# Attention and FFN on one core: each engine's order made with the timeline model

## The chip, the cores and the metric

The program runs on one core of a Trainium2 chip. A core has five engines that work side by side, each through its own list of instructions, strictly in order: TensorE (PE, matrix products), VectorE (DVE), ScalarE (ACT), GpSimd (POOL) and SyncE (SP, which here only issues transfers). They wait for one another by semaphores. The metric is the time of one execution on the device in microseconds (us), as the median of several runs.

## The reference

The input is a batch of 8, with 8 heads, 576 tokens and 64 numbers per head. Every head gets two softmax attentions, one among neighbours (a band of |distance| < 4) and one over the sequence pooled by 4. Their sum, as a matrix of 4608 tokens by 512, goes through a feed-forward network with a piecewise quadratic activation.

```python
q_d, k_d, v_d = mean over groups of 4 tokens of q, k, v
out_up = np.repeat(sm_attn(q_d, k_d, v_d), 4, axis=2)
mask = np.abs(pos[:, None] - pos[None, :]) < 4
scores = np.where(mask, scale * q @ k.T, -1e9)
x = (out_up + softmax(scores) @ v).reshape(4608, 512)
h = x @ w_in                                   # 512 -> 2048
g = np.where(h >= 1, h, np.where(h <= -1, 0, (h + 1) ** 2 / 4))
return g @ w_out                               # 2048 -> 512
```

Everything is float32 except the FFN's weights: they are float64 in the host's memory and the kernel converts them from their two words.

## The kernel before, in words

**Pairs.** Attention works on 32 pairs of two heads: pair n is pair n % 4 of batch n // 4. `attention` is a generator; each `yield` ends a stage, and the stages of a pair run over all engines:

- DVE pools q and k to `qd` and `kd` (L161, L165). PE writes the local scores `sl_ps` (L186) and the pooled scores `sp_ps` (L200). Then SP issues the next pair's q and k loads (L133; `q_sb` and `k_sb` have one buffer each).
- The local softmax: DVE adds the band (L221) and takes the maximum `mxl` (L224), POOL subtracts it (L225), ACT takes the exponential (L226). The pooled one: DVE L236, L237, L238, ACT L240. DVE sums and divides (L249, L250, L253, L254, L258).
- PE transposes the local part, `tl` (L272), which ACT copies to `al` (L276); and the pooled part, `tp` (L284), which ACT copies to `ap` (L290).
- PE multiplies with the values: `pl` (L306) and `pp` (L318). ACT scales `pp` to `xd` (L327), DVE adds to `x` (L329), ACT casts it to `xh` (L336), POOL takes the rest `xl` (L337). `xh` and `xl` are a ring of two batches and the FFN's input, in two parts of less precision.

After the first pairs, `sl_ps`, `tl_ps`, `tp_ps` and `pl_ps` share one PSUM tile (tag a2, one buffer), so that each waits until the one before has been read.

**FFN.** 12 chunks of 384 tokens by 16 slices of the hidden layer make 192 steps, numbered here 0 to 191; h48 is the first product of step 48. A step's first product is 12 matmuls into `h_ps` (L447, two buffers): for each of the four pairs of the batch `xh` twice and `xl` once. ACT takes relu and square (L458, L459), DVE bounds it (L460), which frees `h_ps`; ACT casts to `gh` (L463), POOL takes the rest `gl` (L464). The second product is 9 matmuls into three banks `o_ps` (L478): six from `gh`, three from `gl`. At a chunk's end ACT copies `o_ps` to `osb` (L483), and SP stores it (L484).

A chunk needs all pairs of its tokens' batch. A new batch is needed first at step 16 (pairs 4 to 7), 48 (8 to 11), 64 (12 to 15), 96, 112, 144 and 160 (28 to 31).

**Weights.** SP loads 32 raw slices (L348); ACT (L360, L362, L368), DVE (L365, L366) and POOL (L369) convert them, two for each of the steps 0 to 15.

**What sets the order.** The program emits its work in a hand-written order: `BEFORE_STEPS` and `FIRST_STEPS` for the start, then a loop that emits, for each step, some stages of a pair (`attn_step`), h of a step and the second product of an earlier one. Code under `high_priority` (the activation in `mm1`) is ranked ahead. The library's scheduler then makes the list of each engine from that: it takes the emitted order as a priority and runs a model of the machine to tell which instruction is ready when.

## Time and profile before

| | us |
|---|---|
| median of 2 runs | 1011.65 |
| lowest, highest | 1011.37, 1011.93 |
| span of the profiled execution | 1009.0 |
| mean of PE's clock in it | 0.985 of full |

The span runs from the first to the last instruction; the times of the runs are some 2.65 us longer than it. In the profile a matmul is listed with its tiles, written ahead of `<-`, and its shape; two passes of the array are counted for a matmul of attention, so that the 20 matmuls of L186 appear as 40. Busy time is not the same as need: an engine that works beside PE costs nothing as long as PE does not wait for it. That is why the prediction asks, of each place, what PE stands waiting for.

### The profile page before, as it was taken

To read this page: it belongs to the slowest core of one execution; us is meant where nothing else is said; L and a number is where in the kernel's file an instruction comes from. 1 tells how busy PE (TensorE), PEld (TensorE's weight loads), DVE (VectorE), ACT (ScalarE), POOL (GpSimd) and SP (SyncE) were. 2 spreads that over 40 slices of the span, in tenths; PEclk is the share of its full clock that TensorE was granted. 3 is DMA by queue.
4 is the path that set the end of the run, shared out by engine and by line. 5 is a ranking of instruction groups with operands and counts; after the bars stand their busy time and mean duration, and the time that the engine had idled before them with its cause. 6 is when DMAs were issued, how large, how long until landed. Compare 5 with 4: busy or idle time off the path is not lost.

```text
span 1009.0 us, 18511 instructions
## 1 busy us (share of the span) xinstructions
PE 967.4 (96%) x7612; PEld 845.8 (84%) x7612; DVE 386.9 (38%) x668; ACT 488.3 (48%) x1063; POOL 391.1 (39%) x359
## 2 busy tenths in 40 slices
PE   4688899999999999999999999999999999999997
PEld 4467678998888888998888888999888888899996
DVE  5879872114443443113444434112434444111111
ACT  5678754334545445334445544434544454433433
POOL 3668674224333443222434334222334433222221
PEclk9799899999999999999999999999999999999999
DMA  8685121003112221001221212101212220000000
GB/s 291 212 296 196 50 64 41 1 1 104 50 49 81 74 67 63 1 1 55 73 69 61 75 49 68 39 1 31 74 49 66 91 71 14 32 1 1 32 1 32
DMA packets 26533, 66.24 MB, mean 66 GB/s; under 512 B 3152, under 2 KB 3152, under 8 KB 26448
## 3 DMA queue, kind: packets, MB, share of 16 engines
q1 hardware_dynamic: 26448, 65.06, 19.8%
q8 instruction: 60, 0.98, 0.4%
q14 instruction: 25, 0.20, 0.1%
HBM read 55.61 MB, written 9.44 MB: 64 GB/s over the span
## 4 chain that ended last, share of the span: by engine, by line
PE 79%; DVE 6%; issue 6%; POOL 3%; ACT 3%; DMA 2%; SPq 0%; POOLq 0%; DVEq 0%; ACTq 0%
PE h_ps L447 35%; PE o_ps L478 33%; PE tp_ps L284 2%; PE sl_ps L186 2%; PE pl_ps L306 2%; PE tl_ps L272 2%; DVE m L366 2%; PE pp_ps L318 2%; POOL gl L464 2%; DVE m L365 1%; PE sp_ps L200 1%; DMA first_o<-kT 1%; DMA raw_i<-w_in 1%; POOL sl L225 1%; ACT sp L240 0%
## 5 line engine op out<-in xcount | busy, mean ns | idle before, releaser
L447 PE MATMUL h_ps<-xh,w_i 128*128 128x384 f32 x1536 | 405.7, 344 | 0.0
L464 POOL TENSOR_TENSOR gl<-u,gh 128x384 fp32r<-128x384 f32 x192 | 195.8, 1020 | 525.9 <-ACT gh L463 385.6
L478 PE MATMUL o_ps<-w_o,gh 128*128 128x512 f32 x1152 | 358.2, 392 | 0.4 <-ACT gh L463 0.4
L447 PEld LDWEIGHTS h_ps<-xh,w_i 128*128 128x128 f32 x1536 | 277.0, 188 | 20.8 <-issue 10.9
L460 DVE SCALAR_TENSOR_TENSOR u<-h_ps,u 128x384 f32<-128x384 f32 x192 | 106.8, 556 | 453.4 <-ACT u L459 425.4
L447 PE MATMUL h_ps<-xl,w_i 128*128 128x384 f32 x768 | 262.4, 342 | 0.0
L478 PEld LDWEIGHTS o_ps<-w_o,gh 128*128 128x128 f32 x1152 | 214.2, 188 | 32.6 <-ACT gh L463 1.2
L478 PE MATMUL o_ps<-w_o,gl 128*128 128x512 f32 x576 | 226.2, 393 | 4.3 <-POOL gl L464 4.3
L458 ACT ACTIVATE u<-h_ps 128x384 f32<-128x384 f32 x192 | 94.4, 492 | 271.9 <-PE h_ps L447 271.8
L463 ACT CAST gh<-u 128x384 fp32r<-128x384 f32 x192 | 98.6, 513 | 114.8 <-DVE u L460 114.8
L447 PEld LDWEIGHTS h_ps<-xl,w_i 128*128 128x128 f32 x768 | 144.6, 188 | 0.7 <-POOL xl L337 0.3
L478 PEld LDWEIGHTS o_ps<-w_o,gl 128*128 128x128 f32 x576 | 108.4, 188 | 30.0 <-POOL gl L464 7.1
L459 ACT ACTIVATE u<-u 128x384 f32<-128x384 f32 x192 | 100.3, 523 | 5.0
L225 POOL TENSOR_TENSOR sl<-sl,mxl 128x640 f32<-128x640 f32 x28 | 35.5, 1267 | 43.8 <-DVE mxl L224 43.8
L337 POOL TENSOR_TENSOR xl<-x,xh 128x576 fp32r<-128x576 f32 x32 | 46.4, 1451 | 8.4 <-ACT xh L336 8.4
L329 DVE TENSOR_TENSOR x<-pl_ps,xd 128x576 f32<-128x576 f32 x32 | 24.2, 756 | 59.6 <-ACT xd L327 59.6
L264 POOL TENSOR_TENSOR vh<-vp_sb 72x512 f32<-72x512 f32 x32 | 41.3, 1291 | 10.4 <-DMA vp_sb<-vp 8.3
L221 DVE TENSOR_TENSOR sl<-sl_ps,band_sb 128x640 f32<-128x640 f32 x28 | 23.1, 824 | 41.6 <-PE sl_ps L200 41.6
L249 DVE TENSOR_REDUCE sp_ps<-sl 128x10 f32<-128x640 f32 x32 | 26.4, 825 | 30.1 <-ACT sp L240 30.1
L306 PEld LDWEIGHTS pl_ps<-al,v_sb 64*64 64x64 f32 x1280 | 23.9, 144 | 15.7 <-issue 8.8
L284 PE MATMUL tp_ps<-ident,sp 128*72 128x128 f32 x192 | 29.5, 293 | 4.5 <-ACT sp L240 2.5
L272 PE MATMUL tl_ps<-ident,sl 128*128 128x128 f32 x160 | 25.1, 291 | 8.9 <-POOL sl L254 5.3
(67 smaller groups left out, 777.2 us busy)
## 6 DMA issues: line engine op xcount, KB each, us to landing
v_sb<-vw SPq DMA_DIRECT2D x32, 320.0 KB
vp_sb<-vp SPq DMA_DIRECT2D x32, 288.0 KB
out<-osb SPq DMA_DIRECT2D x36, 256.0 KB
raw_i<-w_in SPq DMA_DIRECT2D x16, 512.0 KB
raw_o<-w_out SPq DMA_DIRECT2D x16, 512.0 KB
q_sb<-qT SPq DMA_DIRECT2D x28, 288.0 KB
k_sb<-kT SPq DMA_DIRECT2D x28, 288.0 KB
first_i<-qT SPq DMA_DIRECT2D x4, 288.0 KB
```

Of the source, the lines that this page charges most:

```text
L225: nc.gpsimd.tensor_tensor(slf, slf, ml_n, op=ALU.subtract)
L272: nc.tensor.transpose(tl_v[:, g * P : (g + 1) * P], sl[:, g].rearrange("p r c -> p (r c)"), ident)
L284: nc.tensor.transpose(tp_v[:, kb, i, :], sp[:, i, kb * KB : (kb + 1) * KB], ident if i < 2 else swapped,)
L306: nc.tensor.matmul(pl_v[hs, o : o + OUT_LEN[i]], v[rs, 2 * g + h, :], al[rs, g, c0 : c0 + OUT_LEN[i]], start=True, stop=True,)
L337: nc.gpsimd.tensor_tensor(xl[:, p, r0 : r0 + S], x, xh[:, p, r0 : r0 + S], op=ALU.subtract)
L447: nc.tensor.matmul(h[:, :TCH], wi[:, wt, cc * P : (cc + 1) * P], xt[:, cc, ts], start=(n == 0), stop=(n == 3 * NCC - 1),)
L458: nc.scalar.activation(u, h[:, :TCH], AF.Relu, bias=0.5, scale=0.5)
L459: nc.scalar.activation(u, u, AF.Square)
L460: nc.vector.scalar_tensor_tensor(u, h[:, :TCH], 1.0, u, op0=ALU.max, op1=ALU.min)
L463: nc.scalar.copy(gh, u)
L464: nc.gpsimd.tensor_tensor(gl, u, gh, op=ALU.subtract)
L478: nc.tensor.matmul(o, gt[:, ts], wo[:, wt, :], start=f == 0 and n == 0, stop=f == NFC - 1 and n == 2)
```

## The change

The scheduler ran with its default model; now it runs with the library's timeline model of the machine. No line of the kernel's work is touched.

```diff
-    with tile.TileContext(nc) as tc:
+    with tile.TileContext(nc, schedule_with_timeline_sim=True) as tc:
         attention_then_ffn(tc, *args, out)
```

Each engine has the same instructions as before, and only their order differs. Three places show how. The names are those of the tiles, with the numbers of their buffers where rows would read alike; x20 counts equal instructions in a row.

PE, before, the end of pair 11, the last that step 48 needs (`h_ps_3145` and `h_ps_3209` are the first products of steps 46 and 47):

```order
L272 MATMUL tl_ps_3128<-ident_73,sl_3043 128x128 x5
L447 MATMUL h_ps_3145<-xh_86,w_i14_1634 128x384 x2
L447 MATMUL h_ps_3145<-xl_87,w_i14_1634 128x384
L447 MATMUL h_ps_3145<-xh_86,w_i14_1634 128x384 x2
L284 MATMUL tp_ps_3136<-ident_73,sp_3049 72x128 x6
L447 MATMUL h_ps_3145<-xl_87,w_i14_1634 128x384
...
L478 MATMUL o_ps2_2425<-w_o13_1585,gl_3116 128x512
L306 MATMUL pl_ps_3175<-al_3134,v_sb_2965 64x61
...
L318 MATMUL pp_ps_3198<-ap_3143,vd_3064 64x144 x4
L447 MATMUL h_ps_3209<-xh_86,w_i15_1697 128x384 x2
```

PE, now, the same pair (`h_ps_3299` is the first product of step 48; its first nine matmuls and those of step 49 stand earlier):

```order
L478 MATMUL o_ps2_2425<-w_o15_1705,gl_3227 128x512
L272 MATMUL tl_ps_3128<-ident_73,sl_3043 128x128 x5
L284 MATMUL tp_ps_3136<-ident_73,sp_3049 72x128 x6
L306 MATMUL pl_ps_3175<-al_3134,v_sb_2965 64x61
...
L318 MATMUL pp_ps_3198<-ap_3143,vd_3064 64x144 x4
L186 MATMUL sl_ps_3242<-k_sb_3041,q_sb_3039 64x64 x20
L200 MATMUL sp_ps_3263<-kd_3240,qd_84 64x144 x2
...
L447 MATMUL h_ps_3299<-xh_86,w_i0_225 128x384 x2
L447 MATMUL h_ps_3299<-xl_87,w_i0_225 128x384
```

The tail of pair 11 and the scores of pair 12 have moved from steps 46 and 48 to one piece between the second product of step 47 and the rest of steps 48 and 49, with no matmul of the FFN in it. Steps 96 (pair 19) and 144 (pair 27) look the same.

DVE, before, from the end of pair 11 on (`u_3222` belongs to step 47, `u_3312` to step 48; `qd` here is that of pair 13):

```order
L329 TENSOR_TENSOR x_3205<-pl_ps_3175,xd_3203 128x576
L165 TENSOR_REDUCE kd_3240<-k_sb_3041 128x144
L460 SCALAR_TENSOR_TENSOR u_3222<-h_ps_3209,u_3222 128x384
L221 TENSOR_TENSOR sl_3274<-sl_ps_3242,band_sb_78 128x640
L236 TENSOR_REDUCE sp_ps_3263<-sl_ps_3242 128x1
L224 TENSOR_REDUCE mxl_3275<-sl_3274 128x10
L237 TENSOR_REDUCE sp_ps_3263<-sp_ps_3263 128x2
L161 TENSOR_REDUCE qd_84<-q_sb_3270 128x144
L238 TENSOR_SCALAR mxp_3281<-sp_ps_3263 128x3
L460 SCALAR_TENSOR_TENSOR u_3312<-h_ps_3299,u_3312 128x384
```

DVE, now:

```order
L329 TENSOR_TENSOR x_3205<-pl_ps_3175,xd_3203 128x576
L165 TENSOR_REDUCE kd_3240<-k_sb_3041 128x144
L221 TENSOR_TENSOR sl_3274<-sl_ps_3242,band_sb_78 128x640
L236 TENSOR_REDUCE sp_ps_3263<-sl_ps_3242 128x1
L161 TENSOR_REDUCE qd_84<-q_sb_3270 128x144
L224 TENSOR_REDUCE mxl_3275<-sl_3274 128x10
L237 TENSOR_REDUCE sp_ps_3263<-sp_ps_3263 128x2
L238 TENSOR_SCALAR mxp_3281<-sp_ps_3263 128x3
L460 SCALAR_TENSOR_TENSOR u_3312<-h_ps_3299,u_3312 128x384
```

`qd` has moved two instructions ahead of the maximum and stands, as before, ahead of L460 of step 48, which PE's step 50 waits for; the score products that release its load are now later on PE. On ACT the relu of a chunk's first step is followed by the three `osb` copies and then by its square.

PE, before, the end of pair 15, the last that step 64 needs (`h_ps_4081` is step 62, `h_ps_4145` step 63, `h_ps_4175` step 64; pair 16 follows at step 79):

```order
L272 MATMUL tl_ps_4064<-ident_73,sl_3979 128x128 x5
L447 MATMUL h_ps_4081<-xh_86,w_i14_1634 128x384 x2
...
L284 MATMUL tp_ps_4072<-ident_73,sp_3985 72x128 x6
...
L318 MATMUL pp_ps_4134<-ap_4079,vd_4000 64x144 x4
L447 MATMUL h_ps_4145<-xh_86,w_i15_1697 128x384 x2
...
L447 MATMUL h_ps_4175<-xh_86,w_i0_225 128x384 x2
```

PE, now, from the end of pair 14 (`pp_ps_3903`) over all of pair 15 to the scores of pair 16 (`sl_ps_4670`); `h_ps_4214` is step 65 and `h_ps_4247` step 66:

```order
L318 MATMUL pp_ps_3903<-ap_3848,vd_3769 64x144 x4
L186 MATMUL sl_ps_3947<-k_sb_3746,q_sb_3744 64x64 x20
...
L447 MATMUL h_ps_4175<-xh_86,w_i0_225 128x384 x2
L447 MATMUL h_ps_4214<-xh_86,w_i1_308 128x384 x2
...
L272 MATMUL tl_ps_4064<-ident_73,sl_3979 128x128 x5
L284 MATMUL tp_ps_4072<-ident_73,sp_3985 72x128 x6
...
L318 MATMUL pp_ps_4134<-ap_4079,vd_4000 64x144 x4
L186 MATMUL sl_ps_4670<-k_sb_3977,q_sb_3975 64x64 x16
...
L447 MATMUL h_ps_4247<-xh_86,w_i2_431 128x384 x2
```

Pair 15, which ended two steps ahead of its need, now begins with its scores when steps 64 and 65 already stand half done, and the only FFN matmuls from there to step 66 are the remaining twelve of steps 64 and 65. Step 112 (pairs 22 and 23) and step 160 (30 and 31) look the same, the latter without a next pair; step 16 has pairs 6 and 7 so.

Two more moves, in words. On SP, at the start, the v load of pair 1 stood 22nd with six of the weight loads ahead of it, and now stands 41st with 25 ahead; the loads of v for pairs 2 and 3 come after it. In the steady steps PE now runs h two steps ahead of the second product, and takes the six `gh` matmuls of it ahead of the three `gl` ones at many steps, where before each bank's three stood together; attention breaks the FFN's matmuls into 136 pieces where there were 117. At the end of the program the second products of steps 189, 190 and 191 all follow h191.

## The prediction

> **What bounds the kernel now.** I read the page first: the busy line, the granted clock by slices, and the chain of work that ended last.
>
> ```profile
> span 1009.0 us, 18511 instructions
> PE 967.4 (96%) x7612; PEld 845.8 (84%) x7612; DVE 386.9 (38%) x668; ACT 488.3 (48%) x1063; POOL 391.1 (39%) x359
> PEclk9799899999999999999999999999999999999999
> PE 79%; DVE 6%; issue 6%; POOL 3%; ACT 3%; DMA 2%; SPq 0%; POOLq 0%; DVEq 0%; ACTq 0%
> ```
>
> TensorE is busy for 967.4 of 1009.0 us and carries 79% of the chain. Then busy time by stage (columns: window, its length, busy time of PE, PEld, DVE, ACT, POOL with counts, PE's clock, DMA share, GB/s).
>
> ```profile
> 0.00:150.00 150.00, 115.65 (x1203) 92.91 (x1204) 118.75 (x176) 103.44 (x224) 96.02 (x82) 0.90 0.55 186
> 25.00:50.00 25.00, 15.67 (x240) 11.40 (x240) 21.27 (x34) 17.01 (x39) 17.03 (x14) 0.70 0.64 209
> 100.00:150.00 50.00, 43.44 (x410) 36.05 (x411) 41.48 (x56) 33.06 (x72) 33.92 (x28) 0.93 0.19 56
> 150.00:952.00 802.00, 799.88 (x6155) 706.65 (x6155) 261.47 (x481) 364.81 (x800) 282.28 (x265) 1.00 0.15 47
> ```
>
> From 150 to 952 us PE misses only 2.1 us: nothing can be won there, and every wait that a new order opens on PE is paid in full. Only the start has air: PE idles 34.4 us of the first 150.
>
> Last the timeline of one ordinary pair of heads in that stretch (start, duration, engine, line, tiles, count). It gives the latency of each link of the attention chain.
>
> ```profile
> 268.94 0.86 PE L186 MATMUL sl_ps<-k_sb,q_sb 64*64 64x64 f32 x38
> 270.28 0.62 PE L447 MATMUL h_ps<-xh,w_i 128*128 128x384 f32 x2
> 274.55 0.52 PE L447 MATMUL h_ps<-xh,w_i 128*128 128x384 f32 x2
> 276.67 0.62 PE L478 MATMUL o_ps<-w_o,gh 128*128 128x512 f32 x2
> 278.71 0.71 PE L272 MATMUL tl_ps<-ident,sl 128*128 128x128 f32 x5
> 279.17 0.60 PE L447 MATMUL h_ps<-xh,w_i 128*128 128x384 f32 x2
> 280.20 0.85 PE L284 MATMUL tp_ps<-ident,sp 128*72 128x128 f32 x6
> 280.81 0.42 PE L447 MATMUL h_ps<-xl,w_i 128*128 128x384 f32 x1
> 284.29 0.80 PE L306 MATMUL pl_ps<-al,v_sb 64*64 64x61 f32 x40
> 285.02 0.71 PE L318 MATMUL pp_ps<-ap,vd 72*64 72x144 f32 x8
> ...
> 270.18 0.82 DVE L221 TENSOR_TENSOR sl<-sl_ps,band_sb 128x640 f32<-128x640 f32 x1 [1.50 <-PE sl_ps L200]
> 271.14 0.81 DVE L224 TENSOR_REDUCE mxl<-sl 128x10 f32<-128x640 f32 x1
> 271.87 0.46 DVE L237 TENSOR_REDUCE sp_ps<-sp_ps 128x2 f32<-128x288 f32 x1
> 273.39 0.75 DVE L161 TENSOR_REDUCE qd<-q_sb 128x144 f32<-128x576 f32 x1 [1.07 <-DMA q_sb<-qT]
> 276.06 0.83 DVE L249 TENSOR_REDUCE sp_ps<-sl 128x10 f32<-128x640 f32 x1 [0.93 <-ACT sp L240]
> 277.42 0.82 DVE L254 TENSOR_TENSOR sl<-sl,sp_ps 128x640 f32<-128x640 f32 x1
> 283.48 0.56 DVE L460 SCALAR_TENSOR_TENSOR u<-h_ps,u 128x384 f32<-128x384 f32 x1 [4.26 <-ACT u L459]
> 286.17 0.76 DVE L329 TENSOR_TENSOR x<-pl_ps,xd 128x576 f32<-128x576 f32 x1 [2.13 <-ACT xd L327]
> ...
> 273.32 0.74 ACT L226 ACTIVATE sl<-sl 128x640 f32<-128x640 f32 x1
> 279.45 0.70 ACT L276 COPY al<-tl_ps 128x640 f32<-128x640 f32 x1 [0.20 <-PE tl_ps L272]
> 281.09 0.64 ACT L290 COPY ap<-tp_ps 72x576 f32<-72x576 f32 x1 [0.94 <-PE tp_ps L284]
> 282.33 0.49 ACT L458 ACTIVATE u<-h_ps 128x384 f32<-128x384 f32 x1 [0.61 <-PE h_ps L447]
> 285.78 0.29 ACT L327 ACTIVATE xd<-pp_ps 128x144 f32<-128x144 f32 x1 [1.19 <-PE pp_ps L318]
> 286.96 0.68 ACT L336 CAST xh<-x 128x576 fp32r<-128x576 f32 x1 [0.89 <-DVE x L329]
> ...
> 272.03 1.26 POOL L225 TENSOR_TENSOR sl<-sl,mxl 128x640 f32<-128x640 f32 x1 [1.68 <-DVE mxl L224]
> 287.74 1.45 POOL L337 TENSOR_TENSOR xl<-x,xh 128x576 fp32r<-128x576 f32 x1
> ...
> 269.90 0.34 SPq L133 DMA_DIRECT2D q_sb<-qT  x1
> ```
>
> Read it as links. tl to tp 1.49 us (280.20 − 278.71, al between). tp to the end of ap 1.53. pl with pp 1.44. From the end of pp (285.73): x is done 1.20 later, xh 1.91, xl 3.46. sl_ps fills in 0.86, the score group holds PE 1.34. The next q load is issued as L186 ends (269.80) and lands 3.59 later, when qd starts. Here all of this lies behind FFN matmuls, which cost 2.12 per 12 (274.55 to 276.67, 0.177 each).
>
> **The change, part by part.** No instruction is added or dropped; only orders change. So I go through PE's new order and ask at each break: how much PE work stands between an instruction and what it needs, and how long does the chain above take? The difference is a wait.
>
> *Light places, steps 48, 96, 144.* tl, tp, pl, pp of the batch's last pair and sl of the next stand together. Start tl at 0: tp 1.49, pl 3.02, pp ends 4.46, x done 5.66, and only then may sl start (one PSUM tile serves both); its L186 part ends 6.52. xl is done at 7.92, so h48 and h49 end near 8.7. But h50 needs the buffer that DVE's L460 for step 48 frees, and DVE now has qd of the next pair ahead of that, behind a load issued at 6.5 that lands at 10.11. Then qd 0.75, L224 0.73, L237 0.46, L460 0.56, with L238 between: h50 starts at 12.7. PE's own work there is tl 0.46, tp 0.61, pl and pp 1.44, sl 1.34, six h 1.06, together 4.9. Wait 7.8, three times: **23.4**. ACT's relu of step 48 ends near 9.2, and the three osb copies now queued ahead of its square take at most al's 0.70 each: square done by 11.9, just before DVE asks for it, so nothing more.
>
> *Heavy places, steps 64 and 112.* Here the last two pairs stand so. From the end of pp[14]: sl[15] at 1.20, L186 ends 2.06, q lands 5.65, qd to 6.40, L224 to 7.21, POOL's subtract 1.26, exp 0.74. From exp's start to L249 it was 2.74 above, with a square and a cast of the FFN between; I take 1.7 without. L249 to the end of L254 is 2.18: tl[15] at 12.4. Then 4.46 to the end of pp, 1.20 to x, sl[16] with four h inside to about 19.6, load 3.59, DVE 2.5: h66 at 25.5. PE work is 7.3. Wait 18.2, twice: **36.4**.
>
> *Step 160.* No q load follows pair 31: sl[31] at 1.20, L221 at 2.44, L224 done 4.21, subtract and exp as before, tl[31] at 9.5, pp ends 13.9, xl 17.4, and relu to L460 1.71 more (282.33 to 284.04): h162 at 19.3. PE work 6.0. Wait **13.3**.
>
> *Step 16.* Pairs 6 and 7 are left to the end likewise. From sl[7] to tl[7] 8.3 us, with 2.8 of PE work; the tail of pair 7 as a light place: 12.2 of waits. Before, the same pairs already left PE idle 6.6 of the 50 us from 100 to 150, which is given back: **5.6**.
>
> *Start.* SP's queue now has 19 more weight loads ahead of pair 1's v.
>
> ```profile
> 27.86 0.33 SPq L139 DMA_DIRECT2D v_sb<-vw  x1
> 60.81 1.00 SPq L348 DMA_DIRECT2D raw_o<-w_out  x1
> 61.86 0.99 SPq L348 DMA_DIRECT2D raw_i<-w_in  x1
> ```
>
> A weight load follows the last by 1.05 us, so that v is issued some 20 us later, near 48; pl of pairs 1 to 3 share one v buffer and follow at a load's 3.6 us each, to about 60. Against that the conversions stand earlier on ACT and fill time. I take **+5**, between −10 and +16.
>
> *Breaks.* PE's FFN runs are broken by attention 136 times where it was 117. The five h from 279.17 to 280.20 took 1.03 instead of 0.885: 0.15 each, **+2.8**. The rest of the FFN order (two h ahead, the six gh before the three gl) keeps each gh and gl behind more PE work than its chain takes: nothing, and if that cover were short by the 0.5 of a cast it would be 0.5 a step. The end, where the last three second matmuls run without an h between: nothing, at most 1 either way.
>
> *Clock.* This row shows what a wait costs beyond itself:
>
> ```profile
> 122.06 1.40 PE L284 MATMUL tp_ps<-ident,sp 128*72 128x128 f32 x6 [1.90 <-ACT al L276]
> 124.54 1.01 PE L447 MATMUL h_ps<-xh,w_i 128*128 128x384 f32 x2
> ```
>
> After 1.90 us idle the same tp takes 1.40 against 0.85 and two h take 1.01 against 0.52: half speed, about 1.9 us lost before it recovers (0.55 on the tp, 0.49 on the two h, the rest on the eight sp between them). In the window 25:50, with PE at 63%, the granted clock was 0.70. The places hold some 11 waits over 1.9 us (one in each light place, two or three in each other): **+21**, between 10 and 27. [...]
>
> *Sum.* 23.4 + 36.4 + 13.3 + 5.6 + 5 + 2.8 + 21 = 107.5. On the span of 1009.0 that is 1116.5. The runs' median, 1011.65, is 2.65 above the span, so 1119, rounded **1120 us**.
>
> **Rivals.**
> - *The places cost less* (1060 to 1095). Engines that wait may answer quicker than in the loaded stretch, and a q load alone may land sooner: 1.5 us at seven loads, a third of the clock term, a start that comes out even.
> - *The start or the clock costs more* (1140 to 1180). The start's upper end (11 more) and the clock's (6 more) give 1137. If all PE work inside the places, some 50 us (three times 4.9, twice 7.3, 6.0 and about 14 at step 16), ran at half speed and lay on the chain, it would be 50 in place of 21: 1149, with the start 1160. For it: 0.70 in 25:50. Against: the slow stretch after 122.06 is short.
> - *Hardly a change* (992 to 1032). The waits would have to be under 20 in sum, four fifths of the chains gone. The links are data, each measured with its waiter idle; only L224 to L249 and the load have slack. Nor is the order the same: the light places have no matmul between tl and tp where before there were five.
> - *Faster* (about 985). The start's idle PE is the only thing to win: 34.4 us, of which early weights and conversions might fill 26. It decides only if the eight places together cost less than what it saves; one light place alone is 7.8 and the two heavy ones 36.
>
> **How the numbers follow.** Forecast 0.60 (1095 to 1145), less 0.20, more 0.10, hardly a change 0.06, faster by over 2% 0.04. 2% is about what a measurement of this kernel can tell from no change. Slower 0.90, same 0.06, faster 0.04. The range of eight in ten leaves out the last two, half of "more" and a little of "less": low 1070 (no clock term beyond 10, start −10, quicker loads), high 1150.
>
> **What would show it.** After: PE idle in front of tl, tp, pl, sl and h at steps 16, 48, 64, 96, 112, 144 and 160, about 8 us at the light ones and 18 at 64 and 112, with DVE's qd waiting for a q load inside; full busy between; PEclk below 9 in those slices; the first h some 5 us later. Wrong if those places show PE busy through, if the idle time lies in the steady steps instead, or if DVE's qd does not wait.

## The result, and the profile after

| | before | after |
|---|---|---|
| median of 2 runs, us | 1011.65 | 1148.25 |
| lowest, highest | 1011.37, 1011.93 | 1147.9, 1148.6 |
| span of the profiled execution | 1009.0 | 1146.8 |
| mean of PE's clock in it | 0.985 | 0.926 |

The kernel became slower: 1.1354 times the time before, with an interval of 1.1326 to 1.1381. The forecast was 1120 with a range of 1070 to 1150, so the time lies in the range, close to its upper end, and 28 us above the forecast. It is where the prediction's second rival ("the start or the clock costs more", 1140 to 1180) was to be.

The page of the changed kernel, the same lines as before: span, busy time, PE's clock in 40 slices, shares of the chain of waits.

```profile
span 1146.8 us, 18502 instructions
PE 1022.5 (89%) x7612; PEld 880.9 (77%) x7612; DVE 381.2 (33%) x668; ACT 482.0 (42%) x1063; POOL 392.3 (34%) x359
...
PEclk7679895999998998899999899699999899879999
...
PE 81%; DMA 7%; DVE 6%; ACT 3%; issue 1%; POOL 1%; SPq 0%; ACTq 0%; DVEq 0%; POOLq 0%
```

In the chain of waits transfers have gone from 2% to 7%. PE's idle time was 41.6 us before (1009.0 less 967.4) and is 124.3 now (1146.8 less 1022.5): 82.7 more. And the same 7612 matmul records keep PE busy 55.1 us longer (1022.5 less 967.4). Together these are the 137.8 by which the span grew. The busy time by stage shows where they are (columns as in the prediction's first such table; the fourth row, 342 to 370, is step 48).

```profile
0.00:158.00 158.00, 117.14 (x1055) 97.28 (x1056) 109.44 (x165) 100.13 (x215) 92.41 (x79) 0.81 0.48 165
158.00:204.00 46.00, 32.15 (x308) 25.76 (x307) 16.73 (x31) 16.26 (x39) 16.35 (x15) 0.74 0.25 77
204.00:342.00 138.00, 138.00 (x938) 119.39 (x937) 33.74 (x62) 54.37 (x117) 42.16 (x40) 1.00 0.11 33
342.00:370.00 28.00, 20.90 (x181) 17.92 (x180) 11.61 (x22) 11.79 (x30) 8.73 (x8) 0.88 0.23 72
...
429.00:478.00 49.00, 32.89 (x309) 26.44 (x309) 16.27 (x30) 15.54 (x38) 14.40 (x13) 0.79 0.22 67
...
975.00:1016.00 41.00, 28.58 (x242) 22.95 (x242) 9.39 (x17) 13.79 (x31) 10.26 (x10) 0.75 0.08 28
```

The rows stand for step 16 (158 to 204), a light place (342 to 370), a heavy one (429 to 478) and step 160 (975 to 1016). PE idles 13.85, 7.10, 16.11 and 12.42 us in them, and its clock is below full there. In between, as from 204 to 342, it does not idle at all. Ahead of 158 us it idles 40.86. So the air is in the start and at the places that the prediction named, and nowhere in the steady steps.

Step 48, all engines, cut to the rows that carry the chain (start, duration, engine, line, tiles; in brackets the idle time before and what ended it; the transposes `tl` and `tp` are listed once for each instruction, the other matmuls of attention twice):

```profile
348.05 0.71 PE L272 MATMUL tl_ps<-ident,sl 128*128 128x128 f32 x5
349.54 0.85 PE L284 MATMUL tp_ps<-ident,sp 128*72 128x128 f32 x6 [0.78 <-ACT al L276]
351.11 0.80 PE L306 MATMUL pl_ps<-al,v_sb 64*64 64x61 f32 x40 [0.72 <-ACT ap L290]
353.81 0.91 PE L186 MATMUL sl_ps<-k_sb,q_sb 64*64 64x64 f32 x40 [1.25 <-DVE x L329]
354.76 0.33 SPq L133 DMA_DIRECT2D q_sb<-qT  x1
355.32 0.61 PE L447 MATMUL h_ps<-xh,w_i 128*128 128x384 f32 x2
358.68 0.75 DVE L161 TENSOR_REDUCE qd<-q_sb 128x144 f32<-128x576 f32 x1 [2.41 <-DMA q_sb<-qT]
360.64 0.55 DVE L460 SCALAR_TENSOR_TENSOR u<-h_ps,u 128x384 f32<-128x384 f32 x1
361.24 1.01 PE L447 MATMUL h_ps<-xh,w_i 128*128 128x384 f32 x2 [4.26 <-DVE u L460]
```

Read it from the last row back (L460's row is that of step 48): h50 waits 4.26 us for DVE's L460; DVE had stood 2.41 us in front of `qd`, for a q load that SP could issue only when the late scores (L186) were through. From tl to h50 it is 13.19 us (361.24 less 348.05), where the prediction had worked out 12.7.

### The profile page after: what moved, and what is told of

Its sections match the earlier page's. It is cut to its first block, busy times and chain, and to the rows that moved or that the text cites. A ratio compares the mean times of both kernels' runs of the same rounds, so it can differ in the third digit from the quotient of the medians.

```text
span 1146.8 us, 18502 instructions
## 1 busy us (share of the span) xinstructions
PE 1022.5 (89%) x7612; PEld 880.9 (77%) x7612; DVE 381.2 (33%) x668; ACT 482.0 (42%) x1063; POOL 392.3 (34%) x359
## 4 chain that ended last, share of the span: by engine, by line
PE 81%; DMA 7%; DVE 6%; ACT 3%; issue 1%; POOL 1%; SPq 0%; ACTq 0%; DVEq 0%; POOLq 0%
PE h_ps L447 36%; PE o_ps L478 34%; DMA vp_sb<-vp 3%; PE sl_ps L186 2%; PE pl_ps L306 2%; DMA q_sb<-qT 2%; DMA raw_o<-w_out 2%; PE pp_ps L318 2%; PE tp_ps L284 2%; PE tl_ps L272 2%; PE sp_ps L200 1%; DVE m L365 1%; DVE m L366 1%; DVE x L329 1%; DVE mxl L224 1%
## 5 line engine op out<-in xcount | busy, mean ns | idle before, releaser
L447 PE MATMUL h_ps<-xh,w_i 128*128 128x384 f32 x1536 | 423.5, 355 | 33.9 <-DVE u L460 31.5
L478 PE MATMUL o_ps<-w_o,gh 128*128 128x512 f32 x1152 | 330.5, 399 | 2.3 <-ACT gh L463 2.3
L447 PEld LDWEIGHTS h_ps<-xh,w_i 128*128 128x128 f32 x1536 | 287.7, 196 | 57.4 <-DVE u L460 33.9
L447 PE MATMUL h_ps<-xl,w_i 128*128 128x384 f32 x768 | 267.3, 350 | 0.8 <-POOL xl L337 0.3
L460 DVE SCALAR_TENSOR_TENSOR u<-h_ps,u 128x384 f32<-128x384 f32 x192 | 106.5, 555 | 483.2 <-ACT u L459 454.3
L478 PE MATMUL o_ps<-w_o,gl 128*128 128x512 f32 x576 | 192.2, 397 | 0.0
L447 PEld LDWEIGHTS h_ps<-xl,w_i 128*128 128x128 f32 x768 | 149.8, 196 | 9.0 <-POOL xl L337 3.5
L329 DVE TENSOR_TENSOR x<-pl_ps,xd 128x576 f32<-128x576 f32 x32 | 24.2, 757 | 127.4 <-ACT xd L327 99.4
L272 PEld LDWEIGHTS tl_ps<-ident,sl 128*128 128x128 f32 x160 | 22.0, 160 | 34.0 <-issue 22.4
L306 PEld LDWEIGHTS pl_ps<-al,v_sb 64*64 64x64 f32 x1280 | 26.8, 152 | 26.3 <-issue 9.7
L306 PE MATMUL pl_ps<-al,v_sb 64*64 64x58 f32 (+3 forms) x1280 | 33.1, 244 | 12.6 <-ACT sp L240 5.9
L186 PEld LDWEIGHTS sl_ps<-k_sb,q_sb 64*64 64x64 f32 x1120 | 24.8, 140 | 25.1 <-DVE x L329 14.6
```

The costliest lines, as they stand in the source:

```text
L186: nc.tensor.matmul(sl_v[x * WIN : (x + 1) * WIN, c : c + WIN], q[hs, w : w + WIN], k[hs, w : w + WIN], start=not early, stop=True, skip_gr ...
L272: nc.tensor.transpose(tl_v[:, g * P : (g + 1) * P], sl[:, g].rearrange("p r c -> p (r c)"), ident)
L306: nc.tensor.matmul(pl_v[hs, o : o + OUT_LEN[i]], v[rs, 2 * g + h, :], al[rs, g, c0 : c0 + OUT_LEN[i]], start=True, stop=True,)
L447: nc.tensor.matmul(h[:, :TCH], wi[:, wt, cc * P : (cc + 1) * P], xt[:, cc, ts], start=(n == 0), stop=(n == 3 * NCC - 1),)
L460: nc.vector.scalar_tensor_tensor(u, h[:, :TCH], 1.0, u, op0=ALU.max, op1=ALU.min)
L478: nc.tensor.matmul(o, gt[:, ts], wo[:, wt, :], start=f == 0 and n == 0, stop=f == NFC - 1 and n == 2)
```

## The experiments

A lag, below, is by how much later than in the kernel before DVE's L460 of a step starts, in the two profiled executions. After the change it is 32.0 us at step 16, 43.9 at 48, 69.7 at 64, 106.2 at 112 and 137.3 at 160. The line numbers of these kernels are a few higher than those above, since lines were added. Each edit is made to the changed kernel or, where it says so, to the experiment named. The library's scheduler is still the one that makes the orders: an edit adds an edge that it has to keep on one engine (`NoSync`: an order of issue, not a wait), and what it does with the other engines then is its own affair. So no edit moves one engine alone: in the first kernel, for instance, DVE's `qd` of step 48 stands behind the maximum again, as in the kernel before. Kernels that are given without a ratio were run once; where a kernel was run four or five times, its times lie 2 to 5 us apart, and smaller differences are not read.

### PE's order at the places

First h was put behind the tail of its pair again: `mark()` remembers PE's last instruction after each call of `attn_step`, and h's first matmul must come behind the last mark but one, its sixth behind the last.

```diff
+            mark()
...
-                nc.tensor.matmul(
+                made = nc.tensor.matmul(
...
+                if n == 0:
+                    behind(made, marks[0])
+                if n == 5:
+                    behind(made, marks[1])
```

> Kept: the timeline model for all engines. Added: edges of issue order on PE alone, from step 16 on, so that a step's first product stays behind the attention emitted ahead of it (its first matmul behind tl, its sixth behind tp; behind sl or pp at the other steps). In the order the places at steps 48, 64, 96, 112, 144 and 160 are gone, step 16 and the finely cut first pairs of every second batch remain. My theory (late attention on PE, its waits and the half clock after them): those six places hold 64.5 us of PE idle and some 32 us of PE time over the usual pitch in the changed kernel, so about 1050 us (1035 to 1065). Rival A (the loss sits in the order of DVE, ACT and in the FFN run two steps ahead, of which all stays): over 1110. Rival B (idle waits alone, the slower matmuls having another cause): about 1084.

Measured: 1061.93 us. Of 136 us of slowdown 86 are gone.

Second, on top of this, the first score matmul of each pair from the eighth on was kept where the program has it.

```diff
+            if n >= 2 * NPAIR and (h, r, g) == SCORE_ORDER[0]:
+                tc.keep_in_program_order(made)
```

> As the first, and the first score matmul of each pair from the third batch on stays behind what was emitted on PE ahead of it, so that pairs 8, 9, 16, 17, 24, 25 are not cut into pieces between FFN matmuls. In the changed kernel the windows with such pairs (204 to 342, 478 to 616, 750 to 889 us) hold 6.5 us of PE time over the usual pitch where the before kernel's holds about 2.8. My theory: 3 times 3.7, so 11 us under the first run, about 1039. Rival (the pieces cost nothing by themselves): as the first run, within 3.

Measured: 1047.28 us. The step was 14.7 and not 11, with the sign and about the size that were expected. It can be seen on PE itself. From L460 of step 47 to that of step 95 PE is busy for 242.74 us in the first kernel and for 237.35 in this one, with the same number of matmul records (1897) and the granted clock at 1.00 in both; so the pieces cost some 5.4 us in 48 steps. Third, on top of both, the same for h's first matmul in steps 0 to 15:

```diff
+                if n == 0 and c == 0:
+                    tc.keep_in_program_order(made)
```

> As the second, and in steps 0 to 15 the first matmul of each first product stays behind all that was emitted on PE ahead of it, so that pairs 6 and 7 end before step 16 as in the kernel before; DVE, ACT, POOL and SP still have the timeline model's order. My theory: the place at step 16 goes with its lag of 30 us, about 1010 (1000 to 1022), the same as the kernel before within 1%. Rival A (the start's new DMA and conversion order costs by itself, 5 to 20 us): 1015 to 1030. Rival B (what remains of the new order of the other engines costs 2% or more): over 1032.

Measured: 1051.38, ratio 1.0396 (1.0376 to 1.0416). This was a miss of 41 us: PE's order in the first steps isn't what the start costs. The busy time by stage of this kernel says where the rest is:

```profile
0.00:182.00 182.00, 120.81 (x1193) 96.92 (x1194) 114.98 (x175) 103.74 (x224) 95.54 (x81) 0.78 0.45 152
182.00:1000.00 818.00, 813.84 (x6207) 715.55 (x6208) 263.16 (x484) 363.10 (x806) 285.94 (x268) 1.00 0.15 46
```

After 182 us PE misses 4.2 us of 818. So with PE's order put back, the places from step 48 on cost next to nothing any more; what is left, some 40 us, is lost before step 16, where the lag is 33. 

Fourth, only the heavy places and step 160 were put back: the changed kernel, with h kept in program order in the fourteen steps ahead of 64, 112 and 160 alone (50 to 63, 98 to 111 and 146 to 159).

```diff
+                if n == 0 and c in (3, 6, 9) and f >= 2:
+                    tc.keep_in_program_order(made)
```

> The timeline model, with the first matmul of each first product behind everything emitted on PE only in steps 50 to 63, 98 to 111 and 146 to 159. In the order the heavy places at 64, 112 and 160 are gone and the light ones at 48, 96 and 144 stay, as does step 16; tl and tp of twelve pairs stand together. My theory: minus 43.7 us idle and 22 us of slow PE time, plus twelve waits of 0.8 us between tl and tp: about 1092 (1080 to 1105). Rival (each of the seven places costs about the same, 17 to 20 us, so three fewer are 55): about 1103 with the twelve waits; a rival by which the places are not the cause: over 1125.

Measured: 1105.33, 43 below the changed kernel and not 56. That is where the rival (each place costs about the same) put it, 1103, though the rows don't show its mechanism. The heavy places went (no jump of the lag at 64, 112 and 160), but the light ones became dearer: from step 47 to 50 the lag grew from 33.5 to 48.9, from 95 to 98 by 20.7 and from 143 to 146 by 20.6. There a second product now followed h48 at once, so that this PE order was not simply the old one in part. It tells the two kinds of place apart only roughly.

### The start

The prediction had seen that SP's queue holds the v load of pair 1 behind 19 more weight loads, and had costed it at 5. Three ways of putting orders of the start back were tried on top of the third kernel.

Weight loads on SP in program order, and the first conversions on ACT too:

```diff
-            nc.sync.dma_start(t, src[f].rearrange("p (n t) -> p n t", t=2))
+            tc.keep_in_program_order(
+                nc.sync.dma_start(t, src[f].rearrange("p (n t) -> p n t", t=2))
+            )
...
-        nc.scalar.activation(high, high, AF.Prelu, scale=2.0**-112, alpha=-(2.0**32))
+        tc.keep_in_program_order(
+            nc.scalar.activation(high, high, AF.Prelu, scale=2.0**-112, alpha=-(2.0**32))
+        )
```

> As the third (1051.4), and two more edges of issue order for the start: each raw weight load stays behind what was emitted on SP ahead of it, and each first conversion on ACT (L360) behind what was emitted on ACT ahead of it. In the order the v loads of pairs 1 to 3 are again ahead of most weight loads, and the exponentials ahead of most conversions. My theory now: the 33 us by which the third run trails the kernel before at step 16 come from the start, where v of pair 1 was issued at 41.5 instead of 27.9 us and ACT, busy 24.8 of the 25 us from 25 to 50 with conversions, let the softmax and with it DVE wait (DVE busy 12.0 instead of 21.3 there). So about 1020 (1012 to 1030). Rival (what is left of the order of DVE and POOL makes the start slow): over 1040.

Measured: 1043.49, ratio 1.0311 (1.0291 to 1.0331). Only a quarter of what was expected came back. With the first half of that edit alone, the loads:

> As the third, with the edge on SP's weight loads alone. If the late v loads are the start's whole loss, the same as the fifth within 4 us; if ACT's early conversions are, as the third, about 1051; I expect most of the gain, since without early loads the conversions cannot be early: 1020 to 1035.

Measured: 1030.36, as expected, and better than with ACT's order too. The lag is 0.3 at step 0 and 0.7 at step 6; it rises to 14.9 at step 8, when weight loads stand behind q loads in SP's queue and DVE is busy only 10.74 of the 25 us from 100 to 125. So the early part of the start is the order on SP, and a new hold-up comes in its place.

Next came milder edges: raw weight loads 3 to 6 of each matrix behind the v load of pair 1, the others behind that of pair 3. Once on the third kernel, once on the changed kernel alone:

```diff
+            v_loads[n] = nc.sync.dma_start(t, vw[b, p].rearrange("k (n d) -> k n d", n=NB)).ins
...
+            if f >= 3:
+                tc.add_manual_dep(
+                    made.ins,
+                    v_loads[1 if f < 7 else 3].name,
```

> As the third (1051.4), and on SP only this: the raw weight loads of slices 3 to 6 stay behind the v load of pair 1, and all later ones behind that of pair 3; nothing holds a weight load behind a q load, which in the fifth and sixth runs kept slices from 7 on waiting. SP's queue then reads nearly as in the kernel before; ACT, DVE and POOL keep the timeline model's order. My theory: the 33 us of the third run's start are the late v loads of pairs 1 to 3 and what they hold up, and the 14 that the sixth run (1030) still lost are its own edges behind the q loads: 1015 to 1022. Rival (the remaining order of ACT and DVE costs as much): 1027 to 1035. Of it some 4 to 6 us come after the start, as in the second to sixth runs.

Measured: 1041.08, ratio 1.0286 (1.0263 to 1.0309). SP issues the v loads of pairs 1 to 3 at 31.9, 39.8 and 52.9 us here, in the third kernel at 41.2, 57.2 and 61.3, in the kernel before at 27.9, 35.2 and 46.7: most of the lateness is gone, not all of it.

> The changed kernel with only those edges on SP's weight loads; PE's places from step 16 on stay in its order. If the start's share is the late v loads: 15 to 30 us under 1148, so 1118 to 1133, with step 16's relu at most 20 us behind the kernel before where it is 32 now. If pairs 6 and 7 are late on PE whatever SP does: 1140 or more.

Measured: 1147.07, no gain that counts. Both missed; the second is in the range that was given for pairs 6 and 7 being late on PE whatever SP does. That v comes late is not by itself what the start costs. Last, the loads in smaller steps (3 to 6 behind the v load of pair 3, 7 to 9 behind that of pair 4, the others behind that of pair 5):

```diff
+                    v_loads[3 if f < 7 else 4 if f < 10 else 5].name,
```

> As the third (1051.4), and on SP the raw weight loads of slices 3 to 6 behind the v load of pair 3, of 7 to 9 behind that of pair 4, of 10 to 15 behind that of pair 5. Nothing is behind a q load. Since conversions follow the loads, ACT then has 9 of the 32 slices converted ahead of the cast of pair 3 (13 in the kernel before, 29 in the changed kernel, 19 in the ninth run, 9 in the sixth) and 22 ahead of that of pair 4 (23; 32; 32; 18). The ninth run made it plain that the v loads alone are not it: u of step 0 came 13 us late with 19 conversions ahead, and DVE waited 24.4 us for ACT's xd. Theory now: the start follows the number of conversions that stand on ACT ahead of the first five pairs, so that this run has u of step 0 within 3 us of the kernel before, step 16 within 10, and 1015 to 1025 in all. Rival (DVE's own order of conversions and softmax, which the edges don't touch, holds the start): step 16 at 14 or more behind, 1028 or more.

Measured: 1039.7, ratio 1.0266 (1.0239 to 1.0294); a miss for the theory, and on the side of its rival. The v loads of pairs 1 to 3 are issued at 31.9, 38.6 and 45.7 us, some 4 us later than before at most. The lag is 1.7 at step 0, 13.2 at step 6, 30.1 at step 10 and 24.2 at step 16. The busy time in pieces of 25 us, of the changed kernel first (two rows), then of this one (four rows), shows what they have in common:

```profile
25.00:50.00 25.00, 15.82 (x151) 11.02 (x151) 12.04 (x25) 24.80 (x58) 7.89 (x6) 0.64 1.03 375
50.00:75.00 25.00, 16.72 (x223) 13.24 (x223) 8.95 (x15) 14.52 (x29) 13.02 (x11) 0.67 0.65 210
```

```profile
50.00:75.00 25.00, 16.82 (x130) 14.00 (x123) 11.97 (x19) 21.44 (x45) 11.30 (x9) 0.66 0.86 311
75.00:100.00 25.00, 19.84 (x177) 15.66 (x176) 20.82 (x32) 14.37 (x33) 13.73 (x11) 1.00 0.12 38
100.00:125.00 25.00, 13.67 (x141) 10.35 (x140) 13.42 (x19) 19.38 (x41) 13.15 (x11) 0.86 0.86 306
125.00:150.00 25.00, 19.77 (x158) 16.71 (x160) 20.45 (x28) 11.12 (x24) 16.06 (x12) 0.85 0.10 32
```

The fifth number is ACT's busy time, the fourth DVE's, the last but one the DMA share. Weight loads come in bunches (shares of 1.03; of 0.86 twice), with each bunch ACT's list is full of conversions (24.80 of 25 us; 21.44 and 19.38), and DVE, which waits for ACT's other work, does little (12.04 and 8.95; 11.97 and 13.42). Before, DVE did 21.27 from 25 to 50. In the changed kernel the wait can be seen itself; these are ACT and then DVE around 50 us:

```profile
48.39 0.69 ACT L360 ACTIVATE raw_o<-raw_o 128x512 f32<-128x512 f32 x1
48.93 0.69 ACT L362 ACTIVATE raw_o<-raw_o 128x512 int32<-128x512 uint32 x1
49.47 0.67 ACT L290 COPY ap<-tp_ps 72x576 f32<-72x576 f32 x1
49.99 0.43 ACT L240 ACTIVATE sp<-sp_ps,mxp 128x144 f32<-128x144 f32 x1
```

```profile
41.87 0.16 DVE L238 TENSOR_SCALAR mxp<-sp_ps 128x3 f32<-128x3 f32 x1
50.51 0.83 DVE L249 TENSOR_REDUCE sp_ps<-sl 128x10 f32<-128x640 f32 x1 [8.47 <-ACT sp L240]
```

DVE had the pooled maximum done at 42.0, and ACT, without a pause, came to the last of that pair's exponentials only at 49.99, since conversions (L360, L362) stood between. The bunches and the low DVE time go together in these two kernels, but not everywhere: in the kernel before, a DMA share of 0.84 from 50 to 75 us goes with 17.54 us of DVE, and in the kernel with the loads alone put back ACT's 23.07 us there go with 17.35. That the bunches cause the whole of the lag was not shown: no kernel put back the orders of SP, ACT and DVE together, and the one with ACT's first conversions put back was slower than the one without.

### The q load in the chain

One chain was cut by itself: in the changed kernel, the `qd` reduce on DVE was kept in program order, which puts it behind L460 of the step at the light places.

```diff
+        if n >= 2 * NPAIR:
+            tc.keep_in_program_order(made)
```

> The changed kernel with the pooled query of the next pair (L161, from the third batch on) behind everything emitted on DVE ahead of it, so that it no longer stands between the band sum and the maximum. The places move (step 48 becomes one of the heavy kind), so the total is no measure: between 1130 and 1165. The measure is the time from the end of pp of pair 11 to the first h of step 50, with the same matmuls between: 8.7 us in the changed kernel (352.56 to 361.24). If the q load binds there, as the prediction had it: 6.5 to 7.3, the rest being the square behind the three osb copies. If the load is hidden by those copies: 8.3 to 8.9.

Measured: 1155.67. PE's rows at step 48 of this kernel:

```profile
356.87 1.23 PE L320 MATMUL pp_ps<-ap,vd 72*64 72x144 f32 x8
359.35 1.44 PE L188 MATMUL sl_ps<-k_sb,q_sb 64*64 64x64 f32 x38 [1.25 <-DVE x L331]
361.79 1.01 PE L449 MATMUL h_ps<-xh,w_i 128*128 128x384 f32 x2
...
362.91 0.84 PE L449 MATMUL h_ps<-xh,w_i 128*128 128x384 f32 x2
...
366.16 0.62 PE L449 MATMUL h_ps<-xh,w_i 128*128 128x384 f32 x2 [2.09 <-DVE u L462]
...
366.80 0.52 PE L449 MATMUL h_ps<-xh,w_i 128*128 128x384 f32 x2
```

From the end of pp (358.10) to h50 it is 8.06 us, where the changed kernel takes 8.68 (352.56 to 361.24). The q load is out of the chain, and the wait fell from 4.26 to 2.09. But PE was at half speed here from tl on, behind a wait of 6.44 us (tl takes 1.30, and 0.71 in the changed kernel; sl 1.44 for 38 records, and 0.91 for 40), and DVE's L462 then waited 1.76 for ACT's square, which stands behind the three `osb` copies. So behind the load stood the square, close by: the prediction had put it at 11.9 of 12.7 us. The 8.06 lies between the two forecasts and meets neither. From the start of sl to h48 it is 2.44 us here and 1.51 in the changed kernel (353.81 to 355.32), so that at full clock some 7.1 would be left, an estimate (8.06 less 2.44, plus 1.51). The kernel as a whole was no faster: 7.4 us above the changed one.

### What half speed costs

To tell a wait from the slow clock after it, matmuls whose results nobody reads were put into the waits. First 40 of them after the second step of each of seven chunks:

```diff
+FILL = 40
+FILL_AT = [(c, 1) for c in (1, 3, 4, 6, 7, 9, 10)]
...
+        if (c, f) in FILL_AT:
+            for _ in range(FILL):
+                tc.keep_in_program_order(
+                    nc.tensor.matmul(h[:, TCH:512], ident, ident, start=True, stop=True)
+                )
```

> The changed kernel with 40 further matmuls of 128 by 128 at the end of the first product of steps 17, 49, 65, 97, 113, 145 and 161, into 128 columns of h_ps that nothing reads, so that PE works through some 4 us of the wait that follows there; they add work and no result. The scheduler moves some steps around them, so the total is the weaker measure. If the slow matmuls behind a wait are the clock's answer to PE's idling: the first 12 h behind the place at step 48, which took 4.01 us in the changed kernel (361.24 to 365.25), take 2.1 to 2.6; in total some 2 us less at each of seven places, about 1135 (1120 to 1148). If they have another cause: 3.5 to 4.2 for the 12, and 1148 or more.

Measured: 1177.11, a miss: 29 above the changed kernel. The other measure was met: the h matmuls behind the place ran at full pitch (18 of them from 378.06 to 381.27 us, or 2.14 for 12). At step 48 PE was already at half speed when they came (two h matmuls took 0.84 at 365.49), and the forty took 9.21 us (two records each), far more than the wait. They were too many, so that the total tells nothing on the clock. The next kernel has 16, and only at the light places (`FILL = 16`, chunks 3, 6 and 9):

> The changed kernel with 16 matmuls of 128 by 128 (some 1.6 us) behind the first product of steps 49, 97 and 145 only, into columns of h_ps that nothing reads, so that the wait of 4.26 us ahead of h50 is cut to some 2.7; all that stands before step 49 is in the changed kernel's order. In the eighth run a wait of 2.09 us was followed by h at full pitch, in the changed kernel one of 4.26 by 12 h in 4.0 us. If the length of the idle stretch decides: the next 12 matmuls of the FFN's first product (those without an interruption) run at 0.18 each, and the total falls by 5 to 8. If not: 0.26 to 0.33 each as now, and the total stays within 3.

Measured: 1138.57, 9.7 below the changed kernel, with more work in it. PE at step 48 (16 matmuls are 32 records):

```profile
359.00 3.73 PE L460 MATMUL h_ps<-ident 128*128 128x128 f32 x32
362.95 0.62 PE L449 MATMUL h_ps<-xh,w_i 128*128 128x384 f32 x2 [0.22 <-DVE u L467]
...
363.58 0.51 PE L449 MATMUL h_ps<-xh,w_i 128*128 128x384 f32 x2
```

The wait, 4.26 before, is filled and h50 runs at full pitch: the next pair of matmuls takes 0.51 us. In the changed kernel the same ones ran so:

```profile
362.05 0.52 PE L447 MATMUL h_ps<-xl,w_i 128*128 128x384 f32 x1
362.37 0.84 PE L447 MATMUL h_ps<-xh,w_i 128*128 128x384 f32 x2
...
364.93 0.52 PE L447 MATMUL h_ps<-xl,w_i 128*128 128x384 f32 x1
365.25 2.31 PE L478 MATMUL o_ps<-w_o,gh 128*128 128x512 f32 x6
...
368.09 0.51 PE L447 MATMUL h_ps<-xh,w_i 128*128 128x384 f32 x2
```

There the granted clock was 0.50 from 360.07 to 366.90; the twelve h matmuls from 361.24 to 365.25 took 4.01 us in place of the 2.12 of an ordinary step, and six second products 2.31 in place of 1.52 (at 346.00). That is 1.9 and 0.8 us, 2.7 together, at one light place, beside the wait. The 9.7 is more than the 5 to 8 expected, and only a part of it is the clock's. By the spans, PE idles 15.6 us less than in the changed kernel: 10.0 less at the light places, where the fillers stand, and 6.4 less at steps 64, 112 and 160, since the scheduler's order behind the fillers differs (a second product stands after four h matmuls of step 50). The fillers themselves take some 11 us of PE, and all other matmuls 5.9 less than before. So the clock gave back 5.9 at most, some 2 us at each light place, an estimate from these sums.

## Why the prediction was right, and where it was short

*PE waits at seven places: right.* The idle time was forecast as 23.4 at the light places and is 20.8 (7.10, 6.90 and 6.77, by the same view as above); 36.4 at the heavy ones and is 31.3 (16.11 and 15.16); 13.3 at step 160 and is 12.42; 12.2 at step 16 and is 13.85. The cause is shown by the rows of these places and by the first two kernels: with PE's order put back there, 86 us went with the first (1148.25 less 1061.93) and 101 with both, and PE idles 10.4 us of the 805 from 180 to 985 in the second. Since DVE's and ACT's orders were made anew with it, this is shown for the order of the places, and not for PE's list apart from theirs.

*The chain of a light place: right.* 13.19 us for 12.7, by the links that were named. The kernel with `qd` late bears out that the load is in it (the wait fell from 4.26 to 2.09) and that the square stands right behind.

*Heavy places: right in kind.* PE at step 64, cut (the last rows of pair 14, pair 15, and h66): the largest wait is that of tl for the softmax of a pair that began too late:

```profile
438.60 0.80 PE L306 MATMUL pl_ps<-al,v_sb 64*64 64x61 f32 x40
453.02 1.30 PE L272 MATMUL tl_ps<-ident,sl 128*128 128x128 f32 x5 [8.53 <-DVE sl L254]
455.10 1.50 PE L284 MATMUL tp_ps<-ident,sp 128*72 128x128 f32 x6 [0.78 <-ACT al L276]
457.32 1.33 PE L306 MATMUL pl_ps<-al,v_sb 64*64 64x61 f32 x40 [0.72 <-ACT ap L290]
...
469.74 1.01 PE L447 MATMUL h_ps<-xh,w_i 128*128 128x384 f32 x2 [3.48 <-DVE u L460]
```

*The clock: too small, and the first step that failed.* The prediction took 21 us from one stretch after one wait of 1.90 us, with 27 as its upper end. These rows show what it missed: from tl at 453.02 on the whole chain is slow (tp 1.50 for 0.85, pl 1.33 for 0.80), with waits of 0.72 to 1.25 us between its pieces; and h is again at 469.74 (1.01 for 0.52), behind a wait of 3.48. Here the whole chain behind one wait of 8.53 is slow, and not 1.9 us of it. The granted clock, read in stretches of 3.41 us, is 0.50 from 448.82 to 465.88, through three stretches in which PE is busy for 1.84, 2.70 and 2.16 us, and comes back after one in which it is busy throughout (the last section has rows). At a light place the chain runs at full speed up to h49, and the clock falls only during the wait of 4.26 (at 360.07). Taking for each stretch PE's busy time less what its matmuls take at their bare pitch in the steady steps, the seven places hold 45 us, some 40 of them above what steady steps of that length would, an estimate; in the stretches of 3.41 us with the granted clock at 0.50 PE is busy there for 73.3 us, half of which is 37. Either is close to double the 21, and nearer to the rival's bound of 50, in which all PE work inside the places ran at half speed. That the rival's 1149 us meets the 1148 measured is partly luck, since its clock was 10 too dear and the breaks and the start made up for it.

*Breaks: too small.* 2.8 was forecast; by the same working the three stretches that follow steps 16, 64 and 112 and are busy throughout hold some 11 us more than such work did before (6.5 each against 2.8). Attention's matmuls stand there in smaller pieces between those of the FFN. The second kernel tests this: with these pairs whole again the time fell by 14.7, and PE's busy time by 5.4 in 48 steps.

*Start and step 16: too small, and the second step that failed.* 5 and 5.6 were forecast. The lag is 17.7 at step 0, falls to about 0 at step 15, while pairs 6 and 7 are left undone and the FFN's steps run ahead of them, and is 32.0 at step 16, which needs them. The prediction priced SP's order by the v load alone, which is issued at 41.5 us and not near 48. It also took 6.6 us off, as idle time before step 16 that the late pairs would give back; but ahead of 158 us PE idles 40.86, where before it idled 34.4 in the first 150. What it left out is that those weight loads bring their conversions to ACT's list ahead of attention ("against that the conversions stand earlier on ACT and fill time"): the rows around 50 us show them holding up exponentials that DVE waits for. With PE's order at step 16 put back, the lag there was 33 all the same, so the loss arises earlier and only shows at 16. Putting the loads back gave 21 of it (1051.38 to 1030.36). Which order of the start on ACT, DVE, POOL and SP holds the rest stays open: late v loads alone don't explain it, and the order of the loads together with that of the first conversions on ACT was put back without success.

*The sum.* The idle terms (23.4, 36.4, 13.3, 5.6 and 5) make 83.7 and came to 82.7, partly by chance: the places from step 48 on were 8.6 below, the start and step 16 above, at 18.2 for 10.6. Clock and breaks, 23.8, came to 55.1; by kind of time the whole error of 30 us is there.

*What would be faster.* No version beat the kernel before; the best of those with the timeline model, at 1030.36 in one run, is 1.9% above it.

## What to carry to other kernels

Where one engine is busy throughout, ask of any new order how much of that engine's work stands between each instruction and what it needs; where a whole chain has none, its latency is paid in full, and can be summed from rows of a steady stretch (12.7 us worked out at step 48, 13.19 measured). Add the slow clock by counting all work between the first long wait and the next stretch without waits, not one stretch for each wait: at step 64 the granted clock was 0.50 from 448.82 to 465.88 us, behind one wait of 8.53. And when loads move ahead, follow them to the engine that consumes them: its list is in order too (around 50 us DVE waited 8.47 for an exponential that stood behind conversions on ACT).

## What the runs showed of the hardware

- PE ran at full speed after a wait of 2.09 us although it had run at half speed up to it (0.84 for two h matmuls at 362.91, 0.52 from 366.80 on, in the kernel with `qd` late). In the kernel before, a wait of 1.90 us was followed by half speed (tp 1.40 for 0.85 at 122.06). So the length of the last wait doesn't decide alone in these rows. The granted clock of the changed kernel, read in short stretches, changed at steps 48 and 64 at 360.07, 366.90, 448.82, 465.88, 469.30 and 472.71 us, which are whole multiples of 3.41 apart. Read in 333 stretches of that length, from 1.67 to 1138.3 us, it is 1.00 in 284 of them and 0.50 in 49, with nothing between. Some of them (window, its length, busy time of PE first, the granted clock third from the end):

```profile
356.66:360.07 3.41, 0.32 (x2) 0.00 (x1) 1.39 (x2) 2.20 (x5) 0.00 (x0) 1.00 0.91 326
360.07:363.48 3.41, 2.24 (x7) 2.24 (x8) 1.08 (x4) 2.40 (x8) 1.27 (x2) 0.50 0.14 53
363.48:366.90 3.42, 3.42 (x11) 3.09 (x10) 3.06 (x7) 2.09 (x6) 2.01 (x2) 0.50 0.00 0
366.90:370.31 3.41, 3.41 (x19) 2.98 (x18) 0.36 (x1) 0.51 (x1) 1.01 (x1) 1.00 0.00 0
...
462.47:465.88 3.41, 3.41 (x23) 2.15 (x25) 0.00 (x0) 0.36 (x1) 0.75 (x1) 0.50 0.28 70
465.88:469.30 3.42, 0.37 (x6) 0.10 (x6) 2.98 (x6) 2.25 (x6) 0.37 (x1) 1.00 0.92 341
469.30:472.71 3.41, 2.98 (x9) 2.98 (x10) 1.00 (x3) 3.32 (x11) 2.67 (x3) 0.50 0.08 29
```

- In these stretches the clock goes with what PE did in the one before. In the changed kernel it fell after fifteen stretches with 0.00 to 2.15 us of PE work (0.32 and 0.37 in the rows above) and stayed full only after stretches with 2.00 or more. It came back after stretches with 2.98 to 3.42 (3.42, 3.41 and 2.98 above) and otherwise stayed at 0.50, after 2.70 or less (2.24 above) and twice after more: after 3.19 at 189.40 and after one with PE busy throughout at the start (32.39 to 35.80). In the kernel before it fell after six with 0.16 to 1.90 (1.51 from 118.79 to 122.20, which holds the wait of 1.90) and stayed full after stretches with 1.93 or more, and once, from 2.73 to 6.15, after one without PE work. In the kernel with `qd` late PE is busy for 1.64 in the 3.41 us up to 367.80, with most of the wait of 2.09, and two h matmuls still take 0.52 at 367.86. So the runs show no sharp limit.
- The return to full speed took no fixed time: some 5.7 us of work after the wait of 4.26 at step 48 (361.24 to 366.90), and 3.0 after the wait of 3.48 at step 66 (469.74 to 472.71, and two h matmuls take 0.52 again at 472.76).
- With sixteen matmuls of 128x128 put into the wait at step 48, PE kept its full pitch there: two h matmuls take 0.51 at 363.58, against 0.84 at 362.37 in the changed kernel. The kernel was 9.7 us faster with them, of which 5.9 at most are the clock's, by the estimate above.
